# Backward of a segment-recurrent attention block: dV rows from TensorE, the tail work in smaller pieces

## The chip, the cores and the metric

The kernel runs on one core of one Trainium2 chip. The time is that of one whole execution on the device in microseconds (us), the median of several runs. The engines of a core that matter here are TensorE (PE; its weight loads are a row of their own, PEld), VectorE (DVE), ScalarE (ACT), GpSimd (POOL), SyncE (SP), and 16 DMA engines that all queues share. Each compute engine works through its own instructions in order. Matmul results land in PSUM, here eight banks of 128 partitions x 512 floats, and DVE or ACT copy them to SBUF.

## The reference, cut to what matters

The forward pass is a recurrence: 2048 rows are cut into 64 segments of 32 rows, each segment is preceded by 8 memory rows, and the first 8 output rows of a segment are the memory of the next. A gated feed-forward block follows. The kernel computes the output and, by reverse differentiation, the gradients of the input, the memory, the weights, the condition and its modulation.

```python
mem = mem0
for s in range(n_seg):                                  # 64 segments
    h = concatenate([mem, x[:, 32 * s:32 * s + 32]])    # 8 + 32 = 40 rows of 512
    q, k, v = (einsum('btd,dhe->bhte', h, W) for W in (Wq, Wk, Wv))   # 32 heads of 128
    p = softmax(where(mask, q @ k^T * scale, -1e9))
    o = einsum('bhte,hed->btd', p @ v, Wo)
    mem = o[:, :8]; outs.append(o[:, 8:])
# out, vjp = jax.vjp(whole block, ...); returned: out and all gradients of grad_out
```

So the backward pass walks the segments from 63 to 0, and each one needs the gradient of its own 8 output memory rows from the segment after it: `dy -> dO -> dP -> dS -> dQ, dK, dV -> dh -> dy` of the segment before.

## The kernel before

The program has stages: the forward recurrence, the feed-forward block forward and backward, weight gradients of that block, the backward recurrence (the loop below), and last the weight gradients of the attention, which read rows of dQ, dK, dV stored to DRAM by the loop. The change is in the loop. Its layouts: 32 heads x 40 rows lie as 11 groups of three heads (`G = 11`), 128 columns to a group; a large result is made in three parts of four, four and three groups (`NP = 3`, `PG = 4`), each in one PSUM bank. The pool `psp` gives six banks in rotation, `psb` two more: one for `dh_ps`, one for the tail.

The helpers. `col_mm` puts four products with only 32 output rows side by side in the array, as four blocks of 32 partitions in one bank; `pair_mm` does so with two heads and two halves of 256 columns. The four blocks have to be added up later ("fold"), which is done by a matmul with a selection matrix after a split in a bf16 high and low part:

```python
def col_mm(self, ps, lhsT, w, n, total):

    j = n % 4
    self.nc.tensor.matmul(ps[32 * j:32 * j + 32, :], lhsT=lhsT, rhs=w, start=(n < 4), stop=(n >= total - 4),
                          tile_position=(0, 32 * j))
# pair_mm: the same for two heads x two halves of 256 columns; four matmuls per pair (cut)
def fold_split(self, pool, ps, name, tags=""):

    parts = []
    for h in range(2):
        sl = slice(256 * h, 256 * h + 256)
        hi = pool.tile([128, 256], BF16, name=name + "_hi", tag=f"{tags}hi{h}", bufs=1)
        nc.scalar.activation(hi[:], ps[:, sl], AF.Copy)
        parts.append(hi)
    for h in range(2):
        lo = pool.tile([128, 256], BF16, name=name + "_lo", tag=f"{tags}lo{h}", bufs=1)
        nc.vector.tensor_tensor(lo[:], ps[:, 256 * h:256 * h + 256], parts[h][:], op=ALU.subtract)
        parts.append(lo)
    return parts

def fold_sum(self, psp, parts, name, tag):

    ft = psp.tile([128, self.cfg.DC, 32], F32, name=name + "_ft", tag=tag)
    for c in range(self.cfg.DC):
        for i in range(2):
            self.nc.tensor.matmul(ft[:, c, :], lhsT=parts[2 * i + c // 2][:, (c % 2) * 128:(c % 2) * 128 + 128],
                                  rhs=self.foldsel[:], start=(i == 0), stop=(i == 1))
    return ft
```

The parts of dQ, dK and dV that belong to a segment's last 8 input rows (32 heads x 8 rows each) are not multiplied with the weights segment by segment. `TailRows` collects them over four segments and does 96 `col_mm` matmuls for all four, in four pieces of 24; the result is folded and stored like dh. `proj_b` is likewise the pass of four segments' last 8 rows of dy through Wo (two halves of 16 matmuls), and `turn_b` transposes its result.

The body of the loop (s is the segment, s4 = s % 4):

```python
def grad_out(nm, xt, pi, eng, ps):
    self.evac(eng, part3(xt, pi), ps[:, 0:min(PG, G - pi * PG), :])
    if pi == NP - 1:
        rows = rxp.tile([128, G, 128], BF16, name="rows_x")
        nc.sync.dma_start(rows[:], xt[:, :], transpose=True)
        dram = {"dVT": self.DVR, "dKT": self.DKR, "dQT": self.DQR}[nm][s]
        row_stores.append(lambda: nc.gpsimd.dma_start(dram, rows[:]))
# ... (cut)
for hf in range(2):
    self.col_pass(psp, WoT, hf, lambda c: dyT[:, c, :], RAd, ("dve", "act")[hf])
    nc.gpsimd.tensor_copy(dOst[0:96, 512 * hf:512 * hf + 512], RAd[0:96, 512 * hf:512 * hf + 512])
if pend:
    pend.pop()()
store_rows_x(1)
# ... (cut) turn(0), turn(1): eight transposes of RAd into dOT
gv0 = grad_mm("dVT", dOst, Pst, 0)
# ... (cut) prod, dp, dost, ds; gv1; dVT parts 0 and 1 emptied by ACT; ds leaves dS on DVE
dht(dVT, WvT, 0)
dht(dVT, WvT, 1)
# ... (cut) to_heads, get_db
store_rows_x(0)
for pi in range(NP):
    dstt(pi)
gks = [grad_mm("dKT", Qst, dS, pi) for pi in range(NP)]
load_rows(Qst_t, self.QST, s - 1)
gv2 = grad_mm("dVT", dOst, Pst, 2)
if s > 0:
    dO_tails(s - 1)
for pi in range(NP):
    grad_out("dKT", dKT, pi, "dve", gks[pi])
grad_out("dVT", dVT, 2, "act", gv2)
self.pop_later()
for pi in range(NP):
    grad_part("dQT", Kst, dST, dQT, pi, "act")
split = tail.split()
load_rows(Kst_t, self.KST, s - 1)
for pi in range(NP):
    dht(dKT, WkT, pi)
dht(dVT, WvT, 2)
if split:
    self.pop_later()
for pi in range(NP):
    dht(dQT, WqT, pi)
parts = self.fold_split(sb2, dh_ps[0], "dh")
tail.collect(s % nseg_t, [dVT, dKT, dQT])
tail.chunk()
ft = self.fold_sum(psp, parts, "dh", "p")
# ... (cut) dy of the next segment, proj_b or turn_b, tail.begin after every fourth segment
```

`grad_mm(nm, lh, rh, pi)` makes one part with a matmul per group, `grad_out` copies it to SBUF, and at the last part issues a DMA transpose of the whole tile on SP and notes a store of the transposed rows to DRAM (a GpSimd DMA of 352 KB). `fold_split` reads 256 columns at a time; `dstt` transposes dS into dST; `pop_later` runs a small deferred transposition and store.

The softmax here doesn't subtract the row's maximum and nothing guards it: scores larger than these inputs give would overflow.

## Time and profile before

| | |
|---|---|
| time, median of 3 (lowest, highest) | 3152.93 us (3149.78, 3154.78) |
| span of the profiled execution | 3149.7 us |
| mean granted TensorE clock | 0.986 |
| busy: PE, PEld, DVE, ACT, POOL | 95%, 54%, 50%, 38%, 47% of the span |
| backward loop (first `WoT,dyT` pass to last `dh_ps`) | 1562.4 to 2568.5 us |
| DMA transposes `rows_x<-dKT`, `<-dVT`, `<-dQT` | 64 each; median 2657, 3284, 1627 ns in SP's queue |

A page of the profile gives busy time by engine, then 40 equal slices of the span with the busy share in tenths, then queues, the chain of work that ended last, and the costliest groups. A group line reads: source line, engine, operation, out<-in by tile names, shapes, count. "L61" and "L63" are the helper that empties PSUM on ACT and DVE, so tiles tell more than lines there. Windows give busy time by engine in any stretch; the timeline lists instructions with start and duration (a run of equal ones has the duration of the whole run); the waits list which instruction sat idle until which other one ended, as total, number and longest.

### The profile page before, as it was taken

Reading aid. Unit: us, or ns where it says so; the run is one execution under the profiler, and the core shown is the slowest. Engines: PE = TensorE matmul, PEld = TensorE weight load, DVE = VectorE, ACT = ScalarE, POOL = GpSimd, SP = SyncE. Lnnn points to the kernel's source line nnn. Section 1 sums busy time; section 2 is a strip of 40 time slices with the busy share of each in tenths; the row PEclk is TensorE's granted clock in tenths of the full one; section 3 lists DMA queues with packets and bytes.
Section 4 is the critical chain, followed back from the end, with each engine's and each line's share of the span. In section 5 each row is a group of like instructions: output and inputs, shape, how many; then the busy total and the mean of one; then the engine's idle time right before and its main releaser. Section 6 shows DMA issues by size and latency. Waiting matters only on the chain.

```text
span 3149.7 us, 97744 instructions
## 1 busy us (share of the span) xinstructions
PE 2980.0 (95%) x39557; PEld 1707.4 (54%) x39557; DVE 1559.5 (50%) x3706; ACT 1188.2 (38%) x2893; POOL 1475.5 (47%) x2974
## 2 busy tenths in 40 slices
PE   5999999999998899989999999999999999999999
PEld 3666666666665344445555555555555544455454
DVE  4556556556555777642255455555555532232321
ACT  2555555555554333312144444444444420010111
POOL 3666666666664566521244444444444432232322
PEclk8999999999999899999999999999999999999999
DMA  9888787787887688897599999999999998666674
GB/s 296 213 213 208 206 214 200 213 215 200 210 211 239 167 214 219 210 277 251 180 240 262 256 264 262 267 268 257 262 251 265 245 288 292 202 199 213 197 232 146
DMA packets 936791, 726.06 MB, mean 231 GB/s; under 512 B 635954, under 2 KB 808530, under 8 KB 935956
## 3 DMA queue, kind: packets, MB, share of 16 engines
q1 hardware_dynamic: 806564, 509.77, 67.9%
q0 software_dynamic: 59120, 148.64, 13.6%
q10 hardware_dynamic: 70656, 61.41, 6.2%
q8 instruction: 311, 5.10, 0.7%
q14 instruction: 140, 1.15, 0.1%
HBM read 294.93 MB, written 276.35 MB: 181 GB/s over the span
## 4 chain that ended last, share of the span: by engine, by line
PE 44%; DMA 5%; issue 4%; ACT 2%; POOL 1%; DVE 1%; SPq 0%; ACTq 0%; POOLq 0%; DVEq 0%
PE dh_ps L216 10%; PE gps L1838 9%; PE pass_ps L254 4%; PE gps5o L1852 4%; PE g_ps L1535 4%; PE gps L1236 3%; PE dh_tps L216 2%; PE tps L1449 2%; PE dp_ps L1514 1%; ACT RAd L61 1%; DMA Kst<-KST 1%; PE dp_ps L1522 1%; PE dh_ft L323 1%; DMA dOst<-RBd 1%; PE turn_ps L1415 1%
## 5 line engine op out<-in xcount | busy, mean ns | idle before, releaser
L1838 PE MATMUL gps<-rows,hrows 128*128 128x512 bf16 (+2 forms) x2160 | 417.5, 355 | 0.0
L1838 PEld LDWEIGHTS <-hrows 128*128 128x128 bf16 x2160 | 211.3, 98 | 204.5
L254 PEld LDWEIGHTS <-hT 128*32 128x32 bf16 x6144 | 158.3, 97 | 161.4 <-issue 2.0
L1564 POOL COPY dOst<-RAd 96x512 bf16<-96x512 bf16 x128 | 78.1, 610 | 354.6 <-DVE RAd L63 344.1
L1842 POOL DMA_DIRECT2D out_dram<-ot x108 | 81.3, 753 | 257.2 <-DVE ot L63 132.3
L877 POOL TENSOR_TENSOR Pst<-Pst,rden 120x1408 bf16<-120x1408 bf16 x63 | 159.6, 2533 | 60.0 <-issue 36.9
L63 DVE CAST ot<-gps 128x512 bf16<-128x512 f32 (+3 forms) x76 | 48.1, 633 | 279.0 <-PE gps L1838 191.2
L61 ACT ACTIVATE ot<-gps 128x512 bf16<-128x512 f32 (+3 forms) x75 | 41.3, 551 | 352.5 <-PE gps L1838 233.3
L314 DVE TENSOR_TENSOR dh_lo<-dh_ps,dh_hi 128x256 bf16<-128x256 f32 x128 | 48.4, 419 | 242.3 <-ACT dh_hi L310 242.3
L216 PE MATMUL dh_ps<-WvT,dVT 128*32 128x512 bf16 x2048 | 134.9, 382 | 0.0
L254 PE MATMUL pass_ps<-Wv,hT 128*32 128x512 bf16 x2048 | 133.3, 380 | 0.2 <-DVE RA0v L63 0.2
L63 DVE CAST RA0v<-pass_ps 128x512 bf16<-128x512 f32 x128 | 88.5, 692 | 89.8 <-PE pass_ps L254 86.2
L1852 PE MATMUL gps5o<-WoT,rows 128*128 128x512 bf16 x592 | 130.0, 382 | 2.4 <-DMA rows<-OSR 2.4
L1524 DVE SCALAR_TENSOR_TENSOR dS<-dp_ps,Pst_l 128x512 bf16<-128x512 f32 (+1 forms) x192 | 112.2, 640 | 38.1 <-PE dp_ps L1522 38.0
L254 PE MATMUL pass_ps<-WoT,dyT 128*32 128x512 bf16 x2048 | 121.9, 380 | 5.2 <-ACT dyT L1623 5.2
L61 ACT ACTIVATE dVT<-g_ps 128x512 bf16<-128x512 f32 (+1 forms) x192 | 107.8, 562 | 45.5 <-PE g_ps L1535 22.7
L254 PE MATMUL pass_ps<-Wk,hT 128*32 128x512 bf16 x2048 | 122.8, 382 | 1.5 <-ACT hT L867 1.1
L224 PE MATMUL at_ps<-Wo,OT 128*32 128x256 bf16 x4096 | 124.0, 274 | 0.1
L216 PE MATMUL dh_ps<-WkT,dKT 128*32 128x512 bf16 x2048 | 123.7, 384 | 0.0
L216 PE MATMUL dh_ps<-WqT,dQT 128*32 128x512 bf16 x2048 | 121.7, 379 | 0.0
L254 PE MATMUL pass_ps<-Wq,hT 128*32 128x512 bf16 x2048 | 121.6, 379 | 0.0
L63 DVE CAST dKT<-g_ps 128x512 bf16<-128x512 f32 (+1 forms) x192 | 112.2, 640 | 2.0 <-PE g_ps L1535 0.4
(413 smaller groups left out, 6885.3 us busy)
## 6 DMA issues: line engine op xcount, KB each, us to landing
OSR<-Ost SPq DMA_DIRECT2D x64, 352.0 KB
OT<-OT SPq DMA_DIRECT2D x64, 352.0 KB
VT<-VTr SPq DMA_DIRECT2D x64, 352.0 KB
PS<-Pst SPq DMA_DIRECT2D x64, 352.0 KB
OT_l<-OT SPq DMA_DIRECT2D x64, 352.0 KB
Pst_l<-PS SPq DMA_DIRECT2D x64, 352.0 KB
VT_l<-VT SPq DMA_DIRECT2D x64, 352.0 KB
DKR<-rows_x POOLq DMA_DIRECT2D x64, 352.0 KB, 5.3
```

The costliest lines, as they stand in the source:

```text
L61: return nc.scalar.activation(out, in_, AF.Copy)
L63: return nc.vector.tensor_copy(out, in_)
L216: self.nc.tensor.matmul(ps[32 * j:32 * j + 32, :], lhsT=lhsT, rhs=w, start=(n < 4), stop=(n >= total - 4), tile_position=(0, 32 * j))
L224: nc.tensor.matmul(ps[32 * j:32 * j + 32, :], lhsT=x[k], rhs=w[k][:, 256 * d:256 * d + 256], start=(n == 0), stop=(n == total - 1), tile_p ...
L254: self.nc.tensor.matmul(ps[32 * j:32 * j + 32, :], lhsT=lhs(c), rhs=rhs, start=(c == 0), stop=(c == DC - 1), tile_position=(0, 32 * j))
L877: nc.gpsimd.tensor_tensor(Pst[0:120, :, :], Pst[0:120, :, :], rden[:, :].unsqueeze(2).to_broadcast([120, G, 128]), op=ALU.mult)
L1236: nc.tensor.matmul(ps[:], lhsT=h2r[:, j, c * 128:(c + 1) * 128], rhs=xr[:, j, :], start=(j == 0), stop=(j == NT - 1))
L1524: nc.vector.scalar_tensor_tensor(out=part3(dS, pi), in0=ps[:, 0:n, :], scalar=cfg.scale, in1=part3(Pst, pi), op0=ALU.mult, op1=ALU.mult)
L1535: nc.tensor.matmul(ps[:, j, :], lhsT=lh[:, g * GW:(g + 1) * GW], rhs=rh[:, g * GW:(g + 1) * GW], start=True, stop=True)
L1838: nc.tensor.matmul(ps[:, 0:ng * E], lhsT=hrows[:, tp_, c * 128:(c + 1) * 128], rhs=rows[:, tp_, 0:ng * E], start=(tp_ == 0), stop=(tp_ == ...
L1842: nc.gpsimd.dma_start(outw[c * 128:(c + 1) * 128, h0:h0 + 3 * (ng - 1) + 1:3, :], ot[:, 0:ng * E].rearrange("p (h e) -> p h e", e=E))
L1852: nc.tensor.matmul(pss[gg][:], lhsT=src[0][:, src[1], gg * E:(gg + 1) * E], rhs=dyrows[:, tp_, :], start=(tp_ == order[0]), stop=(tp_ == o ...
```

## The change

The rows of dV are computed as a product of their own, with the two operands of dV^T exchanged (`lhsT=Pst, rhs=dOst`), so dVT needs no DMA transpose; dVT itself stays, since dh needs it. The eleven new matmuls stand next to dV^T's last part, which moves ahead of the dS transposes. The part of dh that comes from dQT goes to a PSUM tile of its own with `pair_mm`, so that the other two thirds are split while it runs. The 96 tail matmuls are cut into seven pieces (16, 24, 8, 8, 16, 8, 16) and the passes of `proj_b` in halves, and they are put in new places: between the pass of dy and the turns, and after the fold. The second half of RAd is computed and emptied as two quarters. Kst's load is issued ahead of dQT's transpose. The stores of rows are taken from their list at other points. The diff, cut to its core:

```diff
-    def col_pass(self, psp, w, hf, lhs, rows, eng):
+    def col_pass(self, psp, w, hf, lhs, rows, eng, ps=None, cs=None, steps=None):
 
         E, DC = self.cfg.E, self.cfg.DC
-        ps = psp.tile([128, 512], F32, name="pass_ps", tag="p")
-        for c in range(DC):
+        a, n = steps or (4 * hf, 4)
+        if ps is None:
+            ps = psp.tile([128, n * E], F32, name="pass_ps", tag="p")
+        for c in cs or range(DC):
             wc = w[:, c, :].rearrange("p (h e) -> p h e", e=E)
             for j in range(4):
-                rhs = wc[:, 12 * hf + j:12 * hf + j + 10:3, :] if j < 3 else wc[:, 24 + 4 * hf:28 + 4 * hf, :]
+                rhs = wc[:, 3 * a + j:3 * (a + n - 1) + j + 1:3, :] if j < 3 else wc[:, 24 + a:24 + a + n, :]
                 self.nc.tensor.matmul(ps[32 * j:32 * j + 32, :], lhsT=lhs(c), rhs=rhs, start=(c == 0), stop=(c == DC - 1),
                                       tile_position=(0, 32 * j))
         if eng is None:
             return ps
-        self.evac(eng, rows[:, 512 * hf:512 * hf + 512], ps[:])
+        self.evac(eng, rows[:, a * E:(a + n) * E], ps[:])
...
-    def fold_split(self, pool, ps, name, tags=""):
+    def fold_split(self, pool, ps, name, home=None):
 
...
+        hi, lo = (pool.tile([128, 512], BF16, name=f"{name}_{x}", tag=x, bufs=1)[:, :] if home is None
+                  else home[:, 512 * i:512 * i + 512] for i, x in enumerate(("hi", "lo")))
+        nc.scalar.activation(hi, ps[:], AF.Copy)
+        nc.vector.tensor_tensor(lo, ps[:], hi, op=ALU.subtract)
+        return hi, lo
+
+    def fold_sum(self, psp, parts, name, tag, pair=()):
 
         ft = psp.tile([128, self.cfg.DC, 32], F32, name=name + "_ft", tag=tag)
-        for c in range(self.cfg.DC):
-            for i in range(2):
...
+        cs = range(self.cfg.DC)
+        mms = [(t[:, c * 128:(c + 1) * 128], self.foldsel[:], c) for t in parts for c in cs]
+        mms += [(t[:, (c % 2) * 128:(c % 2) * 128 + 128], self.foldhalf[:, c // 2, :], c) for t in pair for c in cs]
+        for n, (lhsT, rhs, c) in enumerate(mms):
+            self.nc.tensor.matmul(ft[:, c, :], lhsT=lhsT, rhs=rhs, start=(n == 0), stop=(n >= len(mms) - self.cfg.DC),
+                                  skip_group_check=True)
         return ft
...
-            def proj_b(t, hf):
-                ps = self.col_pass(psp, WoT, hf, lambda c: dbs[t][:, c, :, :].rearrange("p s q -> p (s q)"), None, None)
-                return lambda: self.evac(("act", "dve")[hf], RBds[t % 2][:, 512 * hf:512 * hf + 512], ps[:])
+            def proj_b(t, hf, parts=1):
+                ps = psb.tile([128, 512], F32, name="pass_ps", tag="dh")
+
+                def part(k):
+                    self.col_pass(psp, WoT, hf, lambda c: dbs[t][:, c, :, :].rearrange("p s q -> p (s q)"), None, None, ps,
+                                  range(k * DC // parts, (k + 1) * DC // parts))
+
+                part(0)
+
+                def rest():
+                    for k in range(1, parts):
+                        part(k)
+                    return lambda: self.evac(("act", "dve")[hf], RBds[t % 2][:, 512 * hf:512 * hf + 512], ps[:])
+
+                return rest
...
-            tail = TailRows(self, sb2, psp, psb, 3, "dh", self.DHB, 4)
+            b_rest = []
+            tail = TailRows(self, sb2, psp, psb, 3, "dh", self.DHB, (16, 24, 8, 8, 16, 8, 16), home=dSs[0])
...
-                    if pi == NP - 1:
+                    if pi == NP - 1 and nm != "dVT":
                         rows = rxp.tile([128, G, 128], BF16, name="rows_x")
                         nc.sync.dma_start(rows[:], xt[:, :], transpose=True)
-                        dram = {"dVT": self.DVR, "dKT": self.DKR, "dQT": self.DQR}[nm][s]
+                        dram = {"dKT": self.DKR, "dQT": self.DQR}[nm][s]
                         row_stores.append(lambda: nc.gpsimd.dma_start(dram, rows[:]))
+
+                rv_rows = rxp.tile([128, G, 128], BF16, name="rows_x")
+
+                def rv_out(pi, eng, ps):
+                    n = min(PG, G - pi * PG)
+                    self.evac(eng, rv_rows[:, pi * PG:pi * PG + n, :], ps[:, 0:n, :])
...
+                        self.col_mm(dh_ps[0], X[:, off:off + 32], WT[:, h, :], n_dh[0], 2 * H)
                         n_dh[0] += 1
 
+                def dht_pairs(X, WT):
+                    ps = psp.tile([128, 256], F32, name="dhq_ps", tag="p")
+                    off = lambda h: (h // 3) * GW + (h % 3) * 32
+                    for n in range(H // 2):
+                        hs = (2 * n, 2 * n + 1)
+                        self.pair_mm(ps, [X[:, off(h):off(h) + 32] for h in hs], [WT[:, h, :] for h in hs], n, H // 2)
+                    return ps
+
+                for a, n, eng in ((0, 4, "dve"), (4, 2, "act"), (6, 2, "act")):
+                    self.col_pass(psp, WoT, 0, lambda c: dyT[:, c, :], RAd, eng, steps=(a, n))
                 for hf in range(2):
-                    self.col_pass(psp, WoT, hf, lambda c: dyT[:, c, :], RAd, ("dve", "act")[hf])
                     nc.gpsimd.tensor_copy(dOst[0:96, 512 * hf:512 * hf + 512], RAd[0:96, 512 * hf:512 * hf + 512])
-                if pend:
-                    pend.pop()()
+                b_done = b_rest.pop()() if b_rest else None
+                if s4 < 2:
+                    tail.chunk()
                 store_rows_x(1)
                 if s == 0:
                     self.p5_first()
@@ -1578,6 +1606,8 @@
...
+                if b_done:
+                    b_done()
...
                 dht(dVT, WvT, 0)
                 dht(dVT, WvT, 1)
+                gv2 = grad_mm("dVT", dOst, Pst, 2)
+                gr0 = grad_mm("dV", Pst, dOst, 0)
+                gr1 = grad_mm("dV", Pst, dOst, 1)
+                gr2 = grad_mm("dV", Pst, dOst, 2)
...
-                for pi in range(NP):
-                    dstt(pi)
+                if s > 0:
+                    dO_tails(s - 1)
+                grad_out("dVT", dVT, 2, "act", gv2)
+                rv_out(0, "act", gr0)
+                rv_out(1, "dve", gr1)
+                dstt(0)
+                rv_out(2, "act", gr2)
+                row_stores.append(lambda s=s, rows=rv_rows: nc.gpsimd.dma_start(self.DVR[s], rows[:]))
+                dstt(1)
+                dstt(2)
                 gks = [grad_mm("dKT", Qst, dS, pi) for pi in range(NP)]
                 load_rows(Qst_t, self.QST, s - 1)
-                gv2 = grad_mm("dVT", dOst, Pst, 2)
-                if s > 0:
-                    dO_tails(s - 1)
                 for pi in range(NP):
                     grad_out("dKT", dKT, pi, "dve", gks[pi])
-                grad_out("dVT", dVT, 2, "act", gv2)
                 self.pop_later()
                 for pi in range(NP):
-                    grad_part("dQT", Kst, dST, dQT, pi, "act")
+                    gq = grad_mm("dQT", Kst, dST, pi)
+                    if pi == NP - 1:
+                        load_rows(Kst_t, self.KST, s - 1)
+                    grad_out("dQT", dQT, pi, "act", gq)
                 split = tail.split()
-                load_rows(Kst_t, self.KST, s - 1)
                 for pi in range(NP):
                     dht(dKT, WkT, pi)
                 dht(dVT, WvT, 2)
+                parts = self.fold_split(sb2, dh_ps[0], "dh", dST)
+                pair = self.split_pair(sb2, dht_pairs(dQT, WqT), "dh")
+                tail.collect(s % nseg_t, [dVT, dKT, dQT])
+                tail.chunk()
                 if split:
                     self.pop_later()
-                for pi in range(NP):
-                    dht(dQT, WqT, pi)
-                parts = self.fold_split(sb2, dh_ps[0], "dh")
-                tail.collect(s % nseg_t, [dVT, dKT, dQT])
-                tail.chunk()
-                ft = self.fold_sum(psp, parts, "dh", "p")
+                store_rows_x(2)
+                ft = self.fold_sum(psp, parts, "dh", "p", pair)
...
+                g = s // 4
+                if s >= NS - 2:
+                    proj_b(g - 1, 3 - s4)()()
+                elif s4 == 3 and g > 0:
+                    b_rest.append(proj_b(g - 1, 1, 2))
+                elif s4 == 2:
+                    tail.chunk()
+                elif s4 == 1 and g > 0:
+                    turn_b(g - 1)()
+                elif s4 == 0 and g > 1:
+                    b_rest.append(proj_b(g - 2, 0, 2))
...
-                pend.append(lambda ft=ft, s=s, then=then: self.store_rows(psp, sb2, ft, self.DHA[s], "dh", "p", then))
+                self.store_rows(psp, sb2, ft, self.DHA[s], "dh", "p", then)
```

Cut are: smaller index changes for the pieces of unequal size in `TailRows`, the earlier loads of dy for `proj_b`, and `home=`, which lets the two tail halves of the split live in the dS tile.

## The prediction

> **What bounds the kernel now.** I read four views in this order: the forty slices, the windows, the timeline of one segment, the waits. The change touches only the backward loop of 64 segments (and, by a shared helper, a small step of the forward loop), so the first task is to find the loop. The first `pass_ps<-WoT,dyT` matmul starts at 1562.4 us and the last `dh_ps` one at 2568.5 us: 1006 us of the 3150.
>
> ```profile
> PE   5999999999998899989999999999999999999999
> DMA  9888787787887688897599999999999998666674
> ```
>
> The loop is slices 20 to 32. TensorE is at 9 tenths, and so are the DMA queues: both are suspects. One undisturbed group of four segments (numbers 48 to 45; a segment runs from its first `pass_ps<-WoT,dyT` matmul to the next one) as windows:
>
> ```profile
> 1803.96:1818.70 14.74, 13.98 (x241) 8.48 (x240) 7.95 (x21) 7.08 (x18) 6.85 (x17) 1.00 1.03 269
> 1818.70:1834.76 16.06, 15.58 (x264) 9.22 (x267) 8.73 (x23) 7.09 (x19) 7.10 (x18) 1.00 1.14 255
> 1834.76:1850.22 15.46, 15.06 (x259) 9.03 (x255) 7.65 (x21) 7.24 (x18) 7.41 (x18) 1.00 1.16 259
> 1850.22:1865.12 14.90, 14.47 (x252) 8.90 (x244) 8.22 (x21) 6.77 (x18) 6.84 (x17) 1.00 1.14 263
> ```
>
> After the length come busy PE, PEld, DVE, ACT, POOL, the clock, the DMA share and GB/s. TensorE is busy for 59.09 of 61.16 us; DVE and ACT are half idle. DMA shares above 1 mean packets overlapping in their engines: full, but elastic. These four lengths recur through the loop almost to the hundredth, which a DMA-bound loop would not do. So **TensorE's in-order stream sets the pace**, 61.16 / 4 = 15.29 us a segment. The loop's real mean, from segment 63's start to segment 0's (1562.38 to 2555.87), is 993.5 / 63 = 15.77; the missing 63 x 0.48 = 30 us are disturbed segments. The waits of ACT and PE over the loop name the disturber:
>
> ```profile
> ACT dVT L61 <- DMA rows_x<-dVT: 15.1, 20, 3.5
> PE g_ps L1535 <- DMA Kst<-KST: 7.4, 7, 2.2
> PE turn_ps L1415 <- ACT RAd L61: 23.6, 62, 0.6
> ```
>
> ACT cannot overwrite dVT until its DMA transpose of the segment before is read out (15.1 us in 20 waits), and Kst comes late behind transposes on the same queue. The third line is no disturbance; it recurs in every segment (62 times, 0.4 us).
>
> **What the Trainium skill says.** "TensorE: Matmul & The Clock Gate", section "Wait — 56ns, not 53.3ns?", has 55.6 ns from start to start for 128 columns and a floor of about 25 ns for tiny ones. The trace agrees: 22 `g_ps` matmuls in 1.24 us on the chain of waits are 56 ns each, and the `dh_ft` ones start 0.02 to 0.04 us apart. "DMA: Bandwidth & Descriptors", section "Issuing engines are not separate DMA queues", says that all queues share 16 engines; taking a transpose off one therefore helps loads and stores on the others, as the shares above 1 suggest. "TensorEngine Tiling (Array Packing)", section "PSUM Bottleneck", warns that once TensorE is fast, emptying PSUM can become the bottleneck. No wait of before shows that in the middle of the segment; I expect it after the change.
>
> **The change part by part.** The clean segment 48 (start 1803.96, the 14.74 us one), on TensorE:
>
> ```profile
> 1805.81 0.40 PE L1415 MATMUL turn_ps<-ident,RAd 128*128 128x128 bf16 x4
> 1806.64 0.40 PE L1415 MATMUL turn_ps<-ident,RAd 128*128 128x128 bf16 x4 [0.43 <-ACT RAd L61]
> ...
> 1809.02 1.48 PE L216 MATMUL dh_ps<-WvT,dVT 128*32 128x512 bf16 x24
> 1810.43 0.79 PE L1449 MATMUL tps<-ident,dS 128*128 128x128 bf16 x11
> 1811.06 0.78 PE L1535 MATMUL g_ps<-dS,Qst 128*128 128x128 bf16 x11
> ...
> 1812.54 1.91 PE L216 MATMUL dh_ps<-WkT,dKT 128*32 128x512 bf16 x32
> ...
> 1818.70 0.40 PE L254 MATMUL pass_ps<-WoT,dyT 128*32 128x512 bf16 x4 [0.29 <-ACT dyT L1623]
> ```
>
> The reader is to see the hole before the second turn, the dense middle, and the hole before the next pass. Times below are from the segment's start.
>
> (1) *Spread work and the smaller second half of RAd.* The pass keeps its column count: 16 matmuls of 512 columns, then 32 of 256. In the forward loop 64 `at_ps` matmuls of 256 columns take as long as 32 of 512 here (1.9 us in both timelines), so this costs nothing. The last products are issued at about 1.75; ACT's copy starts 0.27 later, as before (1805.99), and takes 0.38 for 256 columns (the `dh_hi` row) instead of 0.60: RAd is whole at 2.39 instead of 2.62 us. Eight col-tiled matmuls (8 x 54 ns = 0.43 us: 32 from 1812.54 to 1814.28) now stand between the pass and the turns. First turn at 1.75 + 0.43 + 0.1 of drain = 2.28 instead of 1.85, second right behind it at 2.5 instead of 2.68: dOT is complete at about 3.5 us as before. The 0.43 us are **free**. They come from work that stood elsewhere (tail pieces 24, 24, 24, 24 become 16, 24+8, 8+16, 8+16; dyb passes in halves).
>
> (2) *dV rows.* Eleven matmuls x 56 ns = **+0.62 us** of TensorE, straight on its path. They and dVT's last part stand after the 24 dh matmuls, so the dS transposes move from 6.47 to 6.46 + 0.17 + 0.62 = 7.25.
>
> (3) *Emptying PSUM.* The pool has six banks in rotation; the three dKT products take the banks of the three new dV products. ACT now has in a row: dVT's last part (from 6.87: its matmuls end their issue at 6.6, and a copy starts about 0.3 after the last matmul it needs), dV part 0, dST 0, dV part 2, dST 2. Back to back ACT takes one 512-wide copy per 0.5 us (three dQT copies lie in 1.47) and a 384-wide one per 0.4. So dV part 2 is empty at 6.87 + 0.4 + 0.5 + 0.5 + 0.4 + 0.1 = 8.8. The third dKT product could start at 7.87 + 0.45 = 8.3. **Wait +0.5 us.** DVE (dV part 1 done at 8.0, dST 1 at 8.35) is not last. The dKT dh matmuls start at 9.69 instead of 8.58: +1.11, the sum of (2) and (3).
>
> (4) *dQT's part in a PSUM tile of its own.* From there to the next pass before: 18.70 - 12.54 = 6.16. After: 32 + 8 matmuls 2.17, 64 of 256 columns 1.76 (a run of 64 `at_ps` has that), 16 tail matmuls 0.97 with their drain (16 such passes of `hb` take that in the forward loop), 16 fold matmuls instead of 8 in 0.41, and dyT with its two handovers 0.44, beside which eight matmuls now fit: 5.75. The large split (ACT 0.6, DVE 0.7) lies beside the dQT products; only the half split (0.38 + 0.42 by the 256-wide rows) remains at the end, and the 16 tail matmuls cover it. **-0.4 us.**
>
> Sum for the clean one (number 48): 14.74 + 1.11 - 0.41 = 15.44. By number modulo 4, with the same working: 0: 15.45 (was 14.74). 1: 15.45 (14.90; turn_b fits the dyT hole). 2: 24 tail matmuls in the late slot, 15.9 (15.46). 3: the tail's fold no longer waits for its split in mid-stream, only 0.25 us of matmuls, 15.7 (16.06). Together 62.5 against 61.16: **+1.34 us per four, x 16 = +21 us.**
>
> (5) *DMA.* One of three transposes per segment goes, and SP loses a queue slot of 3.28 us (median of the dVT transposes; dKT 2.66, dQT 1.63). The 15.1 us of ACT waits must vanish, and Kst's load is issued ahead of the dQT transpose. Of the 30 us disturbed, 7.4 are the first segment's loads and stay (23.44 us against 16.06). Of the other 23 I take two thirds, **-15 us**. This fraction is chosen, not computed. Net: 3152.9 + 21 - 15 = 3159.
>
> The store of dV from GpSimd replaces one of the same 352 KB. The forward loop's tail split in two instructions instead of four is under a microsecond in all.
>
> **Rivals.** *PSUM wait weaker than worked out* (an ACT copy finishing sooner, a bank free by luck): for it, ACT is busy only 7 of 15 us; without the 0.5 us the 21 shrink by 63 x 0.5 = 31 and the time would be about 3128. *DMA pressure decides*: the DMA digits are full throughout, and one of three transposes is a large relief; if every disturbance went, another 8 us fall. Against it: the clean segments show no DMA wait at all. *ACT becomes the bound*: beyond (3), later dQT copies or dVT's parts could hold the dh matmuls; each added 0.3 us per segment makes +19 us, about 3178. I see no such wait, since dh by dKT and dVT run 2.17 us ahead of dQT's use.
>
> **Range and chances.** The bare sum is 3159. The terms I trust least are the PSUM wait and the DMA fraction, both more likely too pessimistic than too mild, so I move to **3150**, practically where it was. No PSUM wait gives the low end, 3128; ACT holding more gives the high end, 3178. A 2% change is 63 us, twice the largest term above (31 us); so within 2% 0.94, and 0.03 on either side.
>
> **What would show it.** Right: typical segments of 15.4 to 15.9 us with less spread between the four; no wait for `rows_x<-dVT`; the turn waits nearly gone; a new wait of the third dKT product on ACT's copy of the dV rows, about 0.5 us each time; DMA share below 1. Wrong: clean segments under 15.2 us (the PSUM wait or the fold is cheaper), or a new wait in the last third of the segment (dh or fold on ACT), or disturbed segments as frequent as before, which would mean that transposes were not what disturbed them.

## The result and the profile after

| | before | after |
|---|---|---|
| time, median of 4 (lowest, highest) | 3151.36 us (3142.84, 3154.78) | 3126.14 us (3122.48, 3128.97) |
| ratio to before, 95% interval | | 0.9923 [0.99, 0.9946] |
| span of the profiled execution | 3149.7 us | 3125.4 us |
| loop, start of segment 63 to start of segment 0 | 993.5 us, mean 15.77 | 971.1 us, mean 15.415 |
| segments 48 to 45 together | 61.16 us | 61.23 us |

The change is 25 us faster; in the profiled pair, 22 of 24 us lie in the loop. The prediction had 3150 with a low end of 3128, so the time fell 2 us outside its range.

The page's forty slices of the changed kernel:

```profile
PE   5999999999998799989989999999999999999999
DMA  8887788788787798898589999999999998666674
```

Read at this resolution the page has not changed. The gain shows only when the segments are cut out one by one. The windows of segments 48 to 45 of the changed kernel (length, busy PE, PEld, DVE, ACT, POOL, clock, DMA share, GB/s):

```profile
1798.67:1813.77 15.10, 15.10 (x316) 10.80 (x317) 8.95 (x23) 8.37 (x21) 7.06 (x18) 1.00 1.08 260
1813.77:1829.06 15.29, 15.29 (x327) 10.99 (x326) 9.66 (x24) 8.80 (x22) 6.84 (x17) 1.00 1.01 235
1829.06:1844.80 15.74, 15.74 (x326) 11.10 (x326) 9.15 (x24) 7.90 (x20) 7.38 (x18) 1.00 1.02 258
1844.80:1859.90 15.10, 15.10 (x318) 10.96 (x314) 8.40 (x21) 7.88 (x21) 6.81 (x17) 1.00 0.89 217
```

TensorE is now busy for all of the length, where before it had holes of 2.07 us in the four. It does more (316 matmuls where segment 48 had 241), and the four take as long as before: **an undisturbed segment costs the same**, 15.31 against 15.29 us. What went is the disturbed segments. Before, the 62 segments after the first lay some 23 us in all above their undisturbed lengths; now segment after segment has 15.1, 15.3, 15.7 or 15.1 us, but for a few at the two ends, and a single one is longer (16.5). The whole list of TensorE's waits in the loop after its first segment (total, times, longest) is:

```profile
PE g_ps L1547 <- issue: 0.6, 1, 0.6
PE dh_ft L321 <- ACT dh_hi L231: 0.6, 3, 0.2
PE dh_ft L321 <- DVE dh_lo L233: 0.6, 3, 0.2
PE pass_ps L256 <- ACT dyT L1665: 0.6, 2, 0.3
```

The three waits shown of before are gone: the turn's (23.6 us), Kst's (7.4), and on ACT the one for `rows_x<-dVT` (15.1); no wait of ACT ends with a DMA any more. Over 840 us of the loop (1640 to 2480) the DMA share fell from 1.14 to 0.98.

Segment 48 in detail, TensorE's timeline (start, duration of the run of instructions, what it does, count), to be laid beside the one in the prediction:

```profile
1800.95 0.62 PE L1413 MATMUL turn_ps<-ident,RAd 128*128 128x128 bf16 x8
...
1803.61 1.48 PE L216 MATMUL dh_ps<-WvT,dVT 128*32 128x512 bf16 x24
...
1805.20 0.78 PE L1547 MATMUL g_ps<-dOst,Pst_l 128*128 128x128 bf16 x11
1805.82 0.78 PE L1459 MATMUL tps<-ident,dS 128*128 128x128 bf16 x11
1806.43 0.82 PE L1547 MATMUL g_ps<-dS,Qst 128*128 128x128 bf16 x11
1807.09 0.93 PE L1547 MATMUL g_ps<-dST,Kst 128*128 128x128 bf16 x11
1807.94 1.91 PE L216 MATMUL dh_ps<-WkT,dKT 128*32 128x512 bf16 x32
```

and ACT's timeline in the middle of the same segment:

```profile
1805.79 0.59 ACT L61 ACTIVATE rows_x<-g_ps 128x512 bf16<-128x512 f32 x1
1806.27 0.60 ACT L61 ACTIVATE dST<-tps 128x512 bf16<-128x512 bf16 x1
1806.74 0.51 ACT L61 ACTIVATE rows_x<-g_ps 128x384 bf16<-128x384 f32 x1
1807.12 0.52 ACT L61 ACTIVATE dST<-tps 128x384 bf16<-128x384 bf16 x1
```

All eight turns now run without a hole, from 2.28 us after the segment's start. The dV products (the row `g_ps<-dOst,Pst_l`, 11 matmuls) take the predicted 0.62 us from start to the next row's start. The dKT products, eleven at 56 ns, would span 0.78 us as the two rows above them do; they span 0.82, a wait of 0.04. The dQT products span 0.93, a wait of about 0.16 just behind ACT's last copy into dST (1807.12 + 0.52 = 1807.64; the third part starts at 1807.69).

### The profile page after: what moved, and what is told of

It is laid out like the page before. It is cut to its first block, busy times and chain, and to the rows that moved or that the text cites. A ratio compares the mean times of both kernels' runs of the same rounds, so it can differ in the third digit from the quotient of the medians.

```text
span 3125.4 us, 106126 instructions
## 1 busy us (share of the span) xinstructions
PE 3004.2 (96%) x43769; PEld 1838.1 (59%) x43845; DVE 1616.2 (52%) x3738; ACT 1264.6 (40%) x3053; POOL 1473.0 (47%) x2974
## 4 chain that ended last, share of the span: by engine, by line
PE 50%; issue 4%; DMA 2%; POOL 1%; DVE 0%; SPq 0%; ACT 0%; POOLq 0%; DVEq 0%
PE gps L1885 10%; PE dh_ps L216 8%; PE g_ps L1547 6%; PE pass_ps L256 5%; PE gps5o L1899 4%; PE dhq_ps L224 4%; PE gps L1234 3%; PE dh_tps L216 3%; PE dp_ps L1526 2%; PE tps L1459 2%; PE dp_ps L1534 1%; PE turn_ps L1413 1%; PE dh_ft L321 1%; PE gps L1164 1%; PE wtp L1300 1%
## 5 line engine op out<-in xcount | busy, mean ns | idle before, releaser
L1591 POOL COPY dOst<-RAd 96x512 bf16<-96x512 bf16 x128 | 75.4, 613 | 311.3 <-DVE RAd L63 311.1
L256 PE MATMUL pass_ps<-WoT,dyT 128*32 128x256 bf16 (+1 forms) x3072 | 122.4, 308 | 0.9 <-ACT dyT L1665 0.9
L224 PE MATMUL dhq_ps<-WqT,dQT 128*32 128x256 bf16 x4096 | 122.9, 273 | 0.0
L224 PEld LDWEIGHTS <-dQT 128*32 128x32 bf16 x4096 | 109.6, 97 | 15.9
L709 ACT ACTIVATE ET<-st_ps 128x480 bf16<-128x480 f32 (+1 forms) x192 | 96.1, 535 | 42.6 <-ACT qT L61 34.7
```

The costliest lines, as they stand in the source:

```text
L224: nc.tensor.matmul(ps[32 * j:32 * j + 32, :], lhsT=x[k], rhs=w[k][:, 256 * d:256 * d + 256], start=(n == 0), stop=(n == total - 1), tile_p ...
L256: self.nc.tensor.matmul(ps[32 * j:32 * j + 32, :], lhsT=lhs(c), rhs=rhs, start=(c == 0), stop=(c == DC - 1), tile_position=(0, 32 * j))
L709: nc.scalar.activation(part3(ET, pi)[:, 0:n, 0:120], st_ps[:, 0:n, 0:120], AF.Exp, scale=cfg.scale)
```

## The experiments

The diffs are against the changed kernel unless said otherwise. Each time is a median, with its ratio to the kernel before run beside it and the 95% interval.

### What the dV rows cost: the change without them

```diff
-                gr0 = grad_mm("dV", Pst, dOst, 0)     # and gr1, gr2, and their copies
-                row_stores.append(lambda s=s, rows=rv_rows: nc.gpsimd.dma_start(self.DVR[s], rows[:]))
+                row_stores.append(lambda s=s: nc.gpsimd.dma_start(self.DVR[s], rv_zero[:]))
```

This kernel makes no rows of dV in any way and stores zeros in their place, so the gradient of Wv is left out; dVT and dh are computed as before.

> The changed kernel without dV rows: no product, no copy, no transpose; the store to DRAM stays but stores zeros, so the gradient of Wv is left out. It prices the dV rows on TensorE by themselves. Both theories: undisturbed segments of 14.5 us, no disturbed ones, 3126 - 51 = about 3075. If PSUM hand-over were the larger part (0.5 us and not 0.19, as the prediction had it): 14.2 us and about 3056. The difference to the run with dV by DMA again is what the third transpose costs.

Measured: 3081.08 us, 0.9787 [0.9757, 0.9818]. Four undisturbed segments (44 to 41) take 57.94 us against 61.23 in the change: the rows of dV on TensorE cost 3.29 / 4 = 0.82 us a segment. Over 63 segments that is 52 us; the profiled loops differ by 51, the medians of the two kernels by 45. Of the 0.82, 0.62 are the products and 0.2 is waiting. The predicted +1.11 had 0.5 of waiting.

### The dV rows alone, in the kernel before

```diff
+                gv2 = grad_mm("dVT", dOst, Pst, 2)    # moved up, then gr0, gr1, gr2 = dV products
-                    if pi == NP - 1:                  # transposed rows
+                    if pi == NP - 1 and nm != "dVT":
```

> The kernel before with one part done: dV rows by TensorE beside dVT's last part, the first two dV copies and the third placed as in the change, no dVT transpose; tail pieces, RAd halves, dQT's fold and Kst's load order stay as before. Undisturbed segments of before are 15.29 us; plus 0.62 of products and 0.2 of waits is 16.1 us. Theory R: the disturbed segments vanish (at most 5 us stay): 3151 + 51 - 20 = about 3182. Rival O: they stay, about 3202.

Measured: 3170.11 us, 1.0067 [1.0041, 1.0093], slower than before, though less than either theory had it. Segments 48 to 45 take 64.09 us, +0.73 a segment, and only two segments stand out, the long first one and one of 17.67 us soon after it. With two transposes instead of three the disturbances go even with the old tail work and the old order of loads; but 63 x 0.73 = 46 us of TensorE outweigh the 23. The rest of the change then takes the 0.71 us back (16.02 to 15.31).

### dQT's part of dh in a PSUM tile of its own, taken back

```diff
-                        self.col_mm(dh_ps[0], X[:, off:off + 32], WT[:, h, :], n_dh[0], 2 * H)
+                        self.col_mm(dh_ps[0], X[:, off:off + 32], WT[:, h, :], n_dh[0], 3 * H)
-                pair = self.split_pair(sb2, dht_pairs(dQT, WqT), "dh")
+                for pi in range(NP):
+                    dht(dQT, WqT, pi)                  # ahead of fold_split
```

> The changed kernel with the dQT part of dh accumulated in the common PSUM bank again, so the whole 512-wide split stands between the last dh product and the fold (16 tail products still before the fold). The step's working: the split needs 0.43 to start, 0.6 on ACT and 0.7 on DVE before the last four fold products, about 1.75 us after the last dh product is issued, of which the tail's 0.97 cover part; 8 fold products less. Cost about 0.6 us per segment: 3126 + 38 = 3164. Rival (the split is covered by the tail work anyway): 3126 - 13 = 3113.

Measured: 3141.07 us, 0.9979 [0.9969, 0.9989]; segments 48 to 45 in 62.10 us. The tile of its own is worth 0.87 / 4 = 0.22 us a segment, about 14 us; I had expected more, because the tail matmuls that now stand behind it cover much of the split either way. Of the 0.71 us above, the spread work is left with about 0.49.

### Which copy hands its PSUM bank on

The prediction's 0.5 us of waiting came from the belief that the third dKT product takes the bank of the third dV product. The copy of that part is put last here:

```diff
-                rv_out(2, "act", gr2)                  # between dstt(0) and dstt(1)
                 dstt(1)
                 dstt(2)
+                rv_out(2, "act", gr2)
```

> The changed kernel with ACT's copy of dV's third part issued behind the last dST copy instead of before it. It asks how the six PSUM banks are handed on. Theory by release (a new tile takes the bank whose last reader stands first in the program): the third dKT product takes the first dS transpose's bank and does not wait for the dV copies at all; the third dQT product then waits for the moved copy until 9.02 us as it now waits for dST; nothing changes, 3126 within 4. Theory by turn (the prediction's: each tile takes the bank allotted six tiles earlier): the third dKT product waits for the moved copy until 9.0 us, 0.7 to 0.8 us longer in every segment, about 3170. Theory data only (no bank waits): the third dQT product starts 0.15 us earlier, about 3117.

Measured: 3125.7 us, 0.9928 [0.9905, 0.9951]; the four segments have 15.10, 15.29, 15.75 and 15.10 us, as in the change. The timeline of this kernel, TensorE's and then ACT's rows:

```profile
1804.51 0.82 PE L1547 MATMUL g_ps<-dS,Qst 128*128 128x128 bf16 x11
1805.17 0.93 PE L1547 MATMUL g_ps<-dST,Kst 128*128 128x128 bf16 x11
...
1805.20 0.52 ACT L61 ACTIVATE rows_x<-g_ps 128x384 bf16<-128x384 f32 x1
```

The dKT products end their issue at about 1805.1, before the copy of dV's third part even starts at 1805.20. So they do not wait for that bank. What waits for it is the third dQT product. Its operand is complete at 8.58 us into the segment here, yet it starts at 9.02 as in the change, just behind the end of the moved copy (8.97). So the pool does not hand its banks on by turn; a new tile gets one that has been released. The exact order in which the released ones are picked is not shown.

### The place of Kst's load

```diff
-                    if pi == NP - 1:
-                        load_rows(Kst_t, self.KST, s - 1)
                     grad_out("dQT", dQT, pi, "act", gq)
                 split = tail.split()
+                load_rows(Kst_t, self.KST, s - 1)
```

> The changed kernel with Kst's load issued behind dQT's transpose, as before; nothing else. Theory R: two transposes leave enough room, so at most 5 us are lost: 3126 to 3131. Rival O: the waits for Kst of before return, 7 to 12 us: 3133 to 3138, with PE waits on Kst in several segments.

Measured: 3124.76 us, 0.9927 [0.9904, 0.995], no disturbed segment. With two transposes the load's place is indifferent; the removed transpose does it.

### The dV rows by DMA again, the rest of the change kept

First as it stands, then with the store of dV's rows a segment later:

```diff
-                    if pi == NP - 1 and nm != "dVT":
+                    if pi == NP - 1:
-                gr0, gr1, gr2 and their copies, the store from rv_rows
 # second kernel only:
-                store_rows_x(2)
                 ft = self.fold_sum(psp, parts, "dh", "p", pair)
```

> The changed kernel with one part undone: dV rows come from a DMA transpose of dVT again, the eleven TensorE products and their three copies are gone; the spread work, the dQT pair tile and the Kst load order stay. Theory R (relief: the gain of the change is the vanished disturbed segments, and only fewer DMA transposes make them vanish): undisturbed segments fall from 15.31 to about 14.5 us on average (0.62 of products and 0.19 of waits less), but disturbed ones come back, 23 us or more because the same DMA work now has to fit in a shorter segment; 3126 - 51 + 25 to 50 = 3100 to 3125, with waits of ACT on rows_x<-dVT. Rival O (order: the disturbances went because Kst's load is issued ahead of dQT's transpose and the work is spread; the dV products only cost): no disturbance comes back, 3126 - 51 = about 3075.

> As the first run (dV by DMA transpose, all else of the change kept), but GpSimd's store of the dV rows is issued in the next segment, as before the change, instead of at this segment's end. In the first run GpSimd stood 292 us at that store, in front of the copy that the next segment's pass needs, so that run priced the place of the store and not the transpose. Theory R (relief): undisturbed 14.5 us, with disturbed segments for 23 to 60 us: 3098 to 3135; about the time of the change, so the products on TensorE are bought with nothing lost or little won. Rival O (the dV products only cost): no disturbance, about 3075. If it stays near 3206, the transpose and not the place of the store was the cause there.

Measured: 3206.12 us, 1.0186 [1.0159, 1.0214], and 3184.81 us, 1.0116 [1.008, 1.0152]. Both are slower than before and after, though TensorE has 0.82 us less to do in each segment and some segments do take 14.3. The waits of the first one over the loop:

```profile
POOL DVR L1557 <- DMA rows_x<-dVT: 295.2, 58, 9.5
PE g_ps L1547 <- POOL dOst L1585: 49.9, 25, 5.1
```

GpSimd stands in order at a store of dV's rows until their transpose has landed; its copy into dOst is behind that, and TensorE behind the copy. The first kernel therefore confounds two causes. In the second that wait is down to 37.8 us, and something else disturbs. Three more kernels look for it, all with a fourth buffer for transposed rows (paid for by a single buffer for V^T) and the later store:

```diff
-            rxp = ctx.enter_context(tc.tile_pool(name="p4rx", bufs=3, reuse_waits="tile"))
+            rxp = ctx.enter_context(tc.tile_pool(name="p4rx", bufs=4, reuse_waits="tile"))
 # second kernel only: the 11 dV products are made, and nothing reads them
+                for pi in range(NP):
+                    grad_mm("dV", Pst, dOst, pi)
 # third kernel only: transposes and Kst's load in the order of the kernel before
+   dVT's transpose issued after dKT's, load_rows(Kst_t, ...) after dQT's transpose
```

> dV by DMA transpose in the changed kernel, stored a segment later (as in the run before), and a fourth buffer for transposed rows; its room comes from keeping V^T in one buffer, loaded right after its last use. In the run before, SP stood 204 us in 60 waits at the dVT transpose until the store of the last segment's dV had left the same buffer; SP, and behind it GpSimd, works in order. Theory H (head of the queue: the disturbances come from transposes that wait at the head of an in-order queue for a buffer): those waits go, and the loop runs near its undisturbed 14.5 us: 3080 to 3105, faster than the change. Theory R (load: three transposes, three stores and five loads per segment are too much for 16 DMA engines at this pace, whatever the buffers): disturbed segments stay, at least 1 us on average, 3140 or more.

> As the first kernel of this call, with the eleven dV products made on TensorE but never read: the DMA work of before at nearly the pace of the change (14.5 + 0.62 = 15.1 us). It parts the pace from the load. Theory H: 15.1 us almost undisturbed, 3113 to 3123. Theory R, with load over capacity: 15.8 us as in the kernel before, 3150 or more.

> dV by DMA in every segment with the spare buffer (the run at 3216), but SP's order as before the change: dVT's transpose behind dKT's, Kst's load behind dQT's transpose. The same DMA work cost 23 us of disturbances in the kernel before and 150 us in that run. Theory Q (order: three transposes back to back, with no load between them, are what kept it at 23): undisturbed 14.5 us and 20 to 50 us of disturbances, 3095 to 3125. Theory R (load at this pace): 100 us or more stay, 3175 or more.

And as a control the spare buffer in the kernel before and in the change:

> The kernel before with the fourth buffer and the single V^T buffer alone. In it SP stood 38 us in 35 waits of a transpose for the dK store, and ACT 15 us for the dVT transpose. Theory H: half or more of its 23 us of disturbed segments go: 3128 to 3140. Theory R: they stay within 5 us: about 3147 to 3152.

> Control: the changed kernel with the fourth row buffer and the single V^T buffer, dV by TensorE everywhere. Nothing disturbed there that these could mend: 3122 to 3130. If it is near 3114, the alternation was not what made the alternating kernel faster.

| kernel | time | ratio |
|---|---|---|
| dV by DMA, spare buffer | 3216.44 us | 1.0234 [1.0202, 1.0267] |
| the same with products made but not read | 3178.66 us | 1.0111 [1.0084, 1.0139] |
| the same (no products) in the old order | 3153.01 us | 1.0015 [1.0004, 1.0027] |
| before, spare buffer | 3154.66 us | 1.0028 [1.0011, 1.0044] |
| the change, spare buffer | 3125.92 us | 0.9923 [0.9903, 0.9942] |

Missing buffers are not the cause: with the fourth one SP's wait for the store of dV's rows is all but gone (210.2 to 0.3 us in the loop), and the kernel is slower. Nor is a faster pace alone: with the unread products it runs at nearly the change's pace and is still 52 us slower than the change. But pace and order both count. Behind the first segment, the loop exceeds its undisturbed lengths by 147 us in the new order at 14.49 us a segment, by 72 in the new order at 15.10 (the unread products), by 75 in the old order at 14.49, and by some 23 in the kernel before, with the old order at 15.29 and the old tail work. Each of the two halves the loss or better. None of the theories gives these numbers; single disturbed segments show more.

### Where a disturbed segment loses its time

One from the kernel with dV by DMA and a spare buffer (1699.46 to 1718.95, 19.5 us instead of 14.3 to 14.9). TensorE's timeline, then the windows of one microsecond each from the middle of the hole on:

```profile
1699.46 1.14 PE L256 MATMUL pass_ps<-WoT,dyT 128*32 128x512 bf16 x17
1703.93 1.58 PE L256 MATMUL pass_ps<-WoT,dyT 128*32 128x256 bf16 x31 [3.33 <-issue]
```

```profile
1703.46:1704.46 1.00, 0.53 (x19) 0.51 (x22) 0.00 (x0) 0.00 (x0) 0.00 (x0) 0.92 1.00 84
1704.46:1705.46 1.00, 1.00 (x23) 0.92 (x19) 0.00 (x0) 0.38 (x1) 0.00 (x0) 0.50 1.25 335
...
1707.46:1708.46 1.00, 1.00 (x18) 1.00 (x17) 1.00 (x5) 0.76 (x4) 0.55 (x1) 0.87 1.24 355
1708.46:1709.46 1.00, 1.00 (x23) 0.90 (x24) 0.55 (x2) 1.00 (x3) 0.00 (x0) 1.00 1.02 386
```

TensorE stops for 3.33 us in the middle of a pass whose operands it has been reading all along, and the profile names no releaser ("issue"). Two things happen here.

*The clock.* The granted clock (the third figure from the right) then falls to 0.50 and is back four windows later; 1.7 us of work are lost on top of the hole. "TensorE: Matmul & The Clock Gate", section "What's actually happening", says that an idle window of about 3.4 us halves the clock and that a busy one of that length restores it. The trace agrees on the 3.4 us at half clock, here after a hole of 3.33. But shorter holes did it too: in the loops of all kernels here such a stretch followed on all 48 holes of 3 us and longer, on 46 of the 57 from 2 to 3 us, on 8 of the 51 from 1.5 to 2, and on none of the 63 from 1 to 1.5.

*The instructions.* The DMA queues in the stretch of that hole have one packet of a kind that I had ignored:

```profile
q8 instruction: 1, 0.02, 2.0%
```

It is 16 KB long. Over the whole program the page counts such packets under its queues (number, MB, share of 16 engines). Before:

```profile
q8 instruction: 311, 5.10, 0.7%
```

After:

```profile
q8 instruction: 345, 5.65, 0.8%
```

Before has 39557 matmuls and as many weight loads, after 43769 and 43845. Divided by 256 these sums are 309 and 342, within 1% of the packets: queue 8 brings TensorE's own instructions, 256 in a block. In the trace's packet records the block of this hole ends 1.43 us ahead of TensorE's restart. Over six kernels with a third transpose in every or every other segment there are 67 holes above 0.8 us put down to issue, and 64 of them end 1.1 to 1.7 us after such a block (the other three 2.1 to 2.3), while blocks are some 6.5 us apart. Before and after have no such hole at all. TensorE seems to run dry when its next block comes late through DMA engines full of transposes, and the change's kernel is hungrier: from 1586 to 2510 us it fetches 149 blocks where before fetches 115.

That is a coincidence in time, so two kernels tried it. The first (f1) takes the additional matmuls away from the most disturbed kernel (dh by dQT in 32 matmuls of 512 columns, the second half of RAd whole); the second (f2) adds 64 matmuls a segment to the kernel before, in the same columns:

```diff
 # f1, against dV by DMA with a spare buffer
-                for a, n, eng in ((0, 4, "dve"), (4, 2, "act"), (6, 2, "act")):
+                for a, n, eng in ((0, 4, "dve"), (4, 4, "act")):
+   dQT's part of dh in dh_ps[0] again
 # f2, against the kernel before
-                    self.col_pass(psp, WoT, hf, lambda c: dyT[:, c, :], RAd, ("dve", "act")[hf])
+                    self.col_pass(psp, WoT, hf, lambda c: dyT[:, c, :], RAd, ("dve", "act")[hf], 2)
+   and each dKT matmul of dh as two of 256 columns
```

> The third transpose with fewer TensorE instructions: the kernel with dV by DMA and a spare row buffer (3216 us), but dh by dQT in 32 matmuls of 512 columns instead of 64 of 256 (no PSUM tile of its own) and the second half of RAd whole. Per segment about 56 fewer matmuls and as many fewer weight loads, near the number of the kernel before. Theory I (TensorE runs out of instructions: its next 16 KB block of them comes late through the full DMA engines, and long holes lower its clock): the holes put down to issue shrink from 55 us to under 20, the clock losses from 52 us to under 20, and the time falls to 3140-3175 although the steps taken back cost about 15 to 25 us of TensorE. Rival T (the transposed rows and loads come late by themselves, whatever TensorE fetches): the holes stay, and the time rises to 3220-3245.

> The kernel before, unchanged but for 64 more matmuls in a segment at the same TensorE time: the pass through Wo and dh by dKT in twice as many matmuls of half as many columns. Theory I: holes put down to issue, of which the kernel before has none over 0.8 us, appear (10 to 30 us in all, each ending 1.1 to 1.7 us behind a block of TensorE instructions), some with a lower clock, and the time rises to 3160-3195. Rival T: no such holes, 3143-3160.

Measured: f1 3195.42 us, 1.0148 [1.0107, 1.0188]; f2 3174.21 us, 1.0083 [1.005, 1.0117]. In f2 the waits of TensorE that the kernel before does not have are

```profile
PE dh_ps L1568 <- issue: 12.9, 19, 1.3
PE pass_ps L257 <- issue: 9.9, 9, 2.3
```

and of its 11 holes above 0.8 us (14.7 us) nine end 1.3 to 1.5 us after an instruction block, two within 2.4. Its undisturbed shortest segments take 14.8 us against 14.7, so the matmuls themselves are hardly slower. The same TensorE work in more instructions costs 24 us, as expected from late blocks. In f1 the holes go as expected too, from 21 (55.5 us) to 2 (3.4 us). But the time falls only by 21 us, to a value that neither theory had, and the clock still loses 37 us: another wait has taken their place. The waits of TensorE and of GpSimd in f1:

```profile
PE g_ps L1553 <- DMA dOst<-RBd: 66.5, 28, 5.9
...
POOL DKR L1563 <- DMA rows_x<-dKT: 97.7, 43, 5.0
```

The same accounts for all of these kernels, from 1586 to 2510 us (the clock's column is for the whole loop: the length of each segment after the first times what its clock lacks to 1):

| kernel | instruction blocks | holes "issue" over 0.8 us | TensorE waits for dOst<-RBd | GpSimd waits for rows_x<-dKT | lost to the clock |
|---|---|---|---|---|---|
| before | 115 | 0 | 4.8 us | 5.8 us | 3.3 us |
| f2, before with more matmuls | 141 | 14.7 us | 0 | 0.3 us | 5.2 us |
| after | 149 | 0 | 0 | 4.9 us | 0 |
| dV by DMA, later store | 136 | 11.9 us | 54.0 us | 106.0 us | 28.8 us |
| dV by DMA, spare buffer | 131 | 55.5 us | 27.0 us | 75.4 us | 52.5 us |
| the same, old order | 141 | 19.6 us | 6.5 us | 15.0 us | 5.1 us |
| f1, spare buffer, fewer matmuls | 109 | 3.4 us | 66.5 us | 97.7 us | 37.3 us |

For the kernel with the spare buffer, over the whole loop behind the first segment, all waits of TensorE put down to issue, its waits for dOst<-RBd and the clock's loss are 63.1 + 33.0 + 52.5 = 149 us. That is about the 147 us by which this loop exceeds 62 segments of 14.49 us (the mean undisturbed length without dV products, from the first experiment). So **three transposes of 352 KB in such a segment make other, small transfers late**: TensorE's instruction blocks, or the 16 KB rows of dO that GpSimd issues (dOst<-RBd), behind a GpSimd that stands at the store of dK's rows. These rows are late by themselves too: they land a median of 6.6 us after their issue in the kernel before, and of 4.6 us in the same kernel with only the dV rows changed. Most holes of 2 us and more then cost another 1.7 us through the clock. In the old order the three terms are 25.5, 6.5 and 5.1 us, and some 20 us of other waits stand beside them (14.4 of them for Kst); the loop is 72 us shorter, the median 63. That a late dKT transpose holds GpSimd, and GpSimd the rows of dO, is read from these columns; no run took it apart. Nor did a run show that TensorE asks for its block in time and the full DMA engines alone delay it. The kernel before, with the same three transposes and as few instructions as f1, keeps its dK rows in time; it has both the old order and the slower pace, and how the two do it is open.

### dV by TensorE in every other segment

If TensorE pays 0.82 us for what relieves the DMA engines, half the relief may be enough. In the even segments dV's rows come from TensorE, in the odd ones by DMA; once with the change's buffers, once with the spare one, then in the old order and with stores of rows later:

```diff
+                pe_rows = s % 2 == 0
-                    if pi == NP - 1 and nm != "dVT":
+                    if pi == NP - 1 and not (nm == "dVT" and pe_rows):
 # with the spare buffer: p4rx bufs=4, one V^T buffer
 # old order: as above, in odd segments
 # later stores: store_rows_x(1) after the pass dropped, store_rows_x(0) after the dV products
```

> The changed kernel with dV rows by TensorE in even segments and by DMA transpose in odd ones (stored in the next segment there). Undisturbed: the mean of 15.31 and 14.5 = 14.9 us, 3126 - 26 = 3100. Theory R: the DMA engines sit between the two full cases, so some disturbance is left, 0 to 20 us: 3100 to 3120, faster than the change. Rival O: 3100 with no disturbed segment at all.

> dV by TensorE in even segments and by DMA in odd ones, with the fourth buffer and the single V^T buffer. Without it ACT waited 44 us in 26 waits for the store of the odd segment's rows. Theory H: undisturbed 14.9 us, almost nothing lost: 3098 to 3112. Theory R: between the change and the run with dV by DMA everywhere: 10 to 30 us of disturbances, 3110 to 3130.

> The alternating kernel (3114) with SP's order of before in its DMA segments only. Theory Q: its rest of some 18 us of disturbances shrinks, 3098 to 3110. Theory R: no change, 3110 to 3117.

> The alternating kernel with GpSimd's stores of dK and dQ rows issued together behind the small dO loads in mid-segment instead of dK's in front of them: GpSimd stood 38 us in 24 waits at the dK store, with the next dO rows and dy copies behind it. Theory H for this queue: most of the 18 us of disturbances go, 3098 to 3108. Rival (load): no change or slower, since the stores now meet the next transposes, 3112 to 3125.

| kernel | time (lowest, highest) | ratio |
|---|---|---|
| every other segment | 3161.53 us | 1.0048 [1.0034, 1.0063] |
| with a spare buffer | 3113.79 us (3110.16, 3115.65) | 0.9904 [0.9884, 0.9923] |
| the same, old order | 3116.84 us (3108.12, 3120.41) | 0.9889 [0.9866, 0.9913] |
| the same, later stores | 3133.21 us (3122.67, 3139.19) | 0.9938 [0.9918, 0.9958] |

Without the spare buffer ACT waits 40.7 us in 26 waits for the store of dV's rows to release the buffer that the products' copies need, and TensorE 43.0 us behind ACT: here, and only here, the buffer is the cause. With it the kernel is the fastest of all that compute every gradient; it beats both kernels of this case. Next to the change with the same spare buffer, run on the same chip, the version in the old order has 3116.84 us (3108.12 to 3120.41) against 3125.92 (3122.79 to 3129.63): 9 us less, and no run of the one reaches a run of the other. A segment with a transpose and one with products from its windows:

```profile
1777.12:1791.41 14.29, 14.29 (x306) 10.25 (x302) 7.79 (x20) 7.08 (x19) 6.24 (x16) 1.00 0.95 241
1791.41:1806.51 15.10, 15.10 (x316) 10.79 (x317) 8.96 (x23) 8.37 (x21) 7.62 (x19) 1.00 1.14 275
```

The alternation brings the undisturbed mean from 15.31 to 14.90 us and has some 11 us of disturbances in the loop. The order of issue no longer shows; stores that come later do harm. In all, behind the first segment two transposes disturbed no more than a few single segments in any kernel here (one of 16.48 us in the change), three disturbed every kernel, and three and two in turn did so a little.

## Why the prediction was wrong

Its picture was right: TensorE's stream sets the length of a segment, the dV rows cost TensorE more (52 us) than the third transpose had cost the kernel before (23 us), the spread work fills holes, and the transposes were what disturbed. Its result, no change, was wrong because two terms of the sum were mis-sized, both against the change.

**Step (1), the spread work: right.** The turns start at 2.28 us as worked out and run in one piece; dh by dVT starts 4.94 us into the segment (5.06 before), although eight more matmuls stand ahead of it. That is 0.12 us better than "free".

**Step (2), the dV products: right**, +0.62 us.

**Step (3), "Wait +0.5 us": the step that failed most.** It let the third dKT product wait for ACT's copy of dV's third part, and from that followed a start at 8.8 us. The trace has it start at 8.25, just behind the first dST copy (end 8.20), and the kernel with that copy put last runs the same. In place of one wait of 0.5 there are two of 0.04 and 0.16. The mistake was to take six banks as a fixed rotation; they are handed on as they are released. The whole sum of four segments was predicted at 62.5 us and measured at 61.23, which is 1.27 us less; four times the 0.31 us of this step is 1.24, and the misses of steps (1) and (4) nearly cancel. Over 63 segments it is 20 us. The prediction's own sign of being wrong, clean segments under 15.2 us, came with the 15.10 of segment 48.

**Step (4), the tile of its own: right in kind.** From dh by dKT to the next pass it takes 5.83 us (predicted 5.75, before 6.16), -0.33 instead of -0.41. Taking the tile back costs 0.22 us a segment.

**Step (5), "two thirds, -15 us", which the prediction called chosen: too small.** All but about 1 us of the 23 us of disturbance behind the first segment went. The step saw ACT's wait for dVT's transpose and Kst's load as the disturbers, and both waits are gone; but the experiment with Kst's load put back shows that its place was not needed, and the dV rows alone, in the old order, show that the relief of the DMA engines did it. The first segment's long load stayed, as said (23.60 us against 23.44).

Corrected, the prediction's own sum is 3152.9 + 1 - 23 = 3131, with 2 us less behind the loop 3129. The rest, to 3126, is within the spread of the runs before (3142.84 to 3154.78); in the profiled pair the same terms take 3149.7 to 3125.7, where 3125.4 was measured.

**The rivals.** "PSUM wait weaker than worked out" and "DMA pressure decides" both came true, and the first had been worked out at 3128. The range took the two one at a time; both in full would have been 3159 - 31 - 8 = 3120, so the low end of 3128 was too high by the prediction's own figures. The text held the two terms to be the likely pessimistic ones and still moved by only 9 us from the bare sum. "ACT becomes the bound" did not come: apart from the 0.16 us a segment behind dST's last copy, TensorE's list of waits in the loop has only two on ACT, of 0.6 us each in all.

## What to carry to other kernels

Moving work from DMA to a busy TensorE paid here only with something to pay for it: the dV rows alone made this kernel slower (1.0067), the spread work with dV by DMA gained nothing in its best order of issue (1.0015), and only together are they faster. What full DMA engines cost did not show in their average, 1.14 from 1640 to 2480 us both in the kernel before, which loses 23 us, and in the one that loses 147, but in uneven repeats of the same stretch; cut the loop into its segments, take the shortest as the price of the work and the rest as disturbance, and ask of each long one which small transfer came late. When relief is bought with an engine's time, try half of it, with the buffers that the mixture needs.

## What the hardware showed that I had not expected

- TensorE's instructions come by DMA in blocks of 16 KB, 256 instructions each (345 blocks for 87614 matmuls and weight loads). With three transposes in a segment the kernel before lost 24 us when 64 of its matmuls per segment were written as twice as many of half the columns (3174.21 against 3150.43 us): an instruction count can cost time that the engine's busy time does not contain.
- A hole of 3.3 us in TensorE cost another 1.7 us through its clock, 3.4 us at half speed, and 46 of 57 holes of 2 to 3 us did the same. In the most disturbed kernel this came to 52.5 us.
- The change of the order in which three transposes and a load are issued moved the time by 63 us (3216.44 to 3153.01), with the same transfers of the same sizes.
